# Attention, then two mixture-of-experts layers: the all-experts stage in units of two token tiles, and the second routing's logits on TensorE

## The chip, the cores and the metric

The kernel runs on one core of one Trainium2 chip. The metric is the device time of one execution in microseconds (us). The kernel before took 11301.9 us as the median of 3 runs (11297.12 to 11305.45).

## The reference

Three layers follow one another; the output of the first, read as 24576 tokens of 256 numbers, feeds the second, and the output of the second feeds the third.

```python
# u, v: (8, 3072, 256), z: (8, 3072, 64)
attn = np.maximum(z @ z.T / S, 0.0) ** 2
x = u * (attn @ v)                        # -> N = 24576 tokens, D = 256
# all experts: E = 8, F = 1024
P = np.exp(x @ w_gate - (x @ w_gate).max())
for _ in range(8):
    P /= P.sum(1, keepdims=True) + 1e-9
    P /= P.sum(0, keepdims=True) + 1e-9
    P *= N / E
x = sum(P[:, e:e+1] * (np.maximum(x @ w1[e], 0) @ w2[e]) for e in range(E))
# one expert per token
logits = normalised(x) @ normalised(expert_emb).T / tau
idx, gate = logits.argmax(1), softmax(logits).max(1)
out[idx == e] = gate[idx == e] * (np.maximum(x[idx == e] @ w1b[e], 0) @ w2b[e])
```

## The kernel before, in words

Every matrix product works in float16 pairs: a number is split into a high and a low half, and a product is three matmuls, high by high, high by low and low by high (the loop over `(0,0),(0,1),(1,0)` in `product`).

The program has three stages. The attention stage computes the first layer, batch by batch. The **all-experts stage** computes the second layer. The **job stage** runs the third layer over tokens that were sorted by expert through DRAM (`rows_d`).

The change is in the all-experts stage. Its tokens come in 48 tiles of 512, four tiles to a superblock (12 of them). For a superblock the program walks over the 8 experts, over the four tiles, and over 4 pairs `p` of hidden-column blocks; one such step is a *unit* (1536 of them, list `units`). A unit multiplies a 2x2 block matrix of x (two 128-row blocks of D by the two 256-token halves of the tile) with a 2x2 block matrix of w1 by Strassen's scheme in Winograd's form: 7 block products of 3 matmuls each, 256 columns wide. `unit_head` issues four of them (A11, S1, S2, A22) into PSUM banks b0, b2, b1 and b3, `unit_tail` the other three (A12, S4, S3), which accumulate onto b0, b2 and b1. Between them stand the additions of the scheme. ScalarE copies A11 to `c1` (L863) and S1 to `s5` (L865). VectorE makes `u2` (L869), `c12` (L886) and `u3` (L889). `unit_sums` adds `u3` on GpSimd (L895) and VectorE (L896). ReLU and the split into halves are an ACTIVATE (L883, L887, L901) and a VectorE instruction in `low` (L876).

The second product of the layer is `unit_second`, through `second`: for each of the four 128-token blocks one matmul of the high half with both halves of w2, 512 columns (L908), and one of the low half with the high half of w2, 256 columns onto the right part of the bank (L909). The four blocks own the banks o0 to o3. After the fourth unit of a tile and an expert, `evac_begin` takes o0 to o2 through ScalarE, scaled with the gate (L1163), GpSimd adds them to the accumulator (L1184), and `evac_end` adds o3 on VectorE (L1177).

The order of the work is the order in which the program is written; each engine runs its own instructions in that order. In the loop over units, unit k+1's head stands in front of unit k's first second product, and its tail in front of unit k's other one:

```python
        unit_head(k + 1, (lambda: tick_odd(k - 1)) if k else None)
        unit_split(k)
        unit_second(k, 0)
        bg.tick(2 * k, misc=False, skip=("dots",))
        unit_tail(k + 1)
        unit_second(k, 1)
        evac_begin(i, e)        # after the last unit of tile and expert
        unit_sums(k + 1)
        evac_end(i, e)
```

Side work is written as generators in lanes of a `Background` object; a `tick` advances the lanes by one step each. `misc=False` holds back steps that issue matmuls into bank b3 (they are marked `yield MISC`), so that these come only inside a head, between S1 and S2. The lane "x" loads and splits the next superblock's tiles (`load_tile`), "sum" adds the two halves of a finished tile (`tile_sum`), "dots" computes its logits for the second routing (`tile_logits`: 32 VectorE instructions per tile, L1026), and "end" ranks its tokens by expert, splits them and scatters them to `rows_d` (`tile_end`). In the first superblock "end" also runs the eight passes of the first routing (`sinkhorn`) and then `combine_first`, which applies the gates to what was stored without them.

Of the kernel before, what the change touches and what calls it, by code (L numbers as in the profile page):

```python
# [11 lines left out]
P = 128  # L12
# [74 lines left out]
def program(tc, u, v, z, wg, w1a, w2a, emb, tau, w1b, w2b, out, pool, psum, dram):  # L87
# [49 lines left out]
    def all_max(dst, src, n, waits=4):  # L137
# [5 lines left out]
        rows = pool.tile([P, D], F32, name="amax", tag=f"junk{n - 1}", bufs=1)[:, 0:n * P]  # L143
# [357 lines left out]
    def chunk_end(b, qc, osb, ut):  # L501
# [35 lines left out]
        xt = m4([P, 2, 4, 2 * P], F16, "xt")  # L537
        for t in range(4):
            SP.dma_start_transpose(
                out=xt[:, t // 2, :, (t % 2) * P:(t % 2) * P + P], in_=xr[:, t].rearrange("p k a d -> p (k a d)")  # L540
            )
        for _ in range(6):
            yield
        SP.dma_start(out=xT_d[b * QC + qc], in_=xt.rearrange("p h c q -> p (h c q)"))
# [3 lines left out]
        for t in range(4):  # L548
            for c in range(4):
                k, a = divmod(c, 2)  # L550
                x = xt[:, t // 2, c, (t % 2) * P:(t % 2) * P + P]
# [19 lines left out]
    bg.lane("sum")  # L571
    bg.lane("dots")
# [7 lines left out]
        (lp + 2, lp + 3),  # L580
# [18 lines left out]
    def load_tile(i):  # L599

        x = slot(xring[i % 6], [P, 2, 4, 2, 2 * P], F16, "xs")
        SP.dma_start(out=x[:, 0].rearrange("p c a q -> p (c a q)"), in_=xT_d[i])
        yield
        yield
        bx = m4([P, 4, 2 * P], F32, "bx")
        for c in range(4):
            POOL.tensor_tensor(out=bx[:, c], in0=x[:, 0, c, 0], in1=x[:, 0, c, 1], op=ALU.add)
            if c % 2:
                yield
        b11, b21, b12, b22 = (bx[:, c] for c in range(4))  # L610
        POOL.tensor_tensor(out=b11, in0=b12, in1=b11, op=ALU.subtract)
        POOL.tensor_tensor(out=b12, in0=b22, in1=b12, op=ALU.subtract)
        yield
        POOL.tensor_tensor(out=b22, in0=b22, in1=b11, op=ALU.subtract)
        POOL.tensor_tensor(out=b21, in0=b21, in1=b22, op=ALU.subtract)
        yield
        yield
        yield
        for c in range(4):
            ACT.activation(out=x[:, 1, c, 0], in_=bx[:, c], func=AF.Copy)  # L620
            if c:
                DVE.tensor_tensor(out=x[:, 1, c - 1, 1], in0=bx[:, c - 1], in1=x[:, 1, c - 1, 0], op=ALU.subtract)
            yield
        DVE.tensor_tensor(out=x[:, 1, 3, 1], in0=bx[:, 3], in1=x[:, 1, 3, 0], op=ALU.subtract)
        X[i] = x
# [11 lines left out]
    with tc.manual_schedule():  # L637
# [146 lines left out]
        def attn_main(i):  # L784
# [24 lines left out]
            if b == B - 1 and qc == 1 and n == 0:  # L809
                for j in range(SB):  # L810
                    bg.add("x", load_tile(j))
# [650 lines left out]
```

## Time and profile before

| | |
|---|---|
| time, median of 3 runs | 11301.9 us |
| the profiled execution, its own time | 11322.61 us |
| its span | 11320.9 us |
| PE busy | 10696.5 us, 94% of the span, 75264 matmuls |
| PE weight loads busy | 7242.3 us, 64% |
| VectorE (DVE) busy | 8310.0 us, 73% |
| ScalarE (ACT) busy | 5271.1 us, 47% |
| GpSimd (POOL) busy | 5223.5 us, 46% |
| mean granted TensorE clock | 0.987 |

The share of the span says which engine is busiest, averaged over stages with different limits. A matmul's row lasts until its results are out, while the next one has long begun, so the rows of neighbours overlap and a busy PE is not yet PE at its own pace. That pace is read from the starts of successive matmuls in the timeline.

### The profile page before, as it was taken

How to read it: one execution, taken by the hardware profiler on the slowest of the kernel's cores; microseconds unless marked ns; L12 is line 12 of the kernel's file. 1: busy time of each engine (PE TensorE's matmuls, PEld its weight loads, DVE VectorE, ACT ScalarE, POOL GpSimd, SP SyncE). 2: the span in 40 equal slices, each digit the busy share in tenths (PEclk: the TensorE clock that was granted, in tenths of full speed). 3: DMA queues.
4: the chain of work that ended last, by engine and by line, in shares of the span. 5: the costliest groups of instructions: out<-in, count | busy, mean ns of one | idle time of the engine just before them, and what ended most of it. 6: DMA issues, size and time to landing. Idle time of an engine off the chain costs nothing. (4 is left out here: it accounts for less than half of the span.)

```text
span 11320.9 us, 205345 instructions
## 1 busy us (share of the span) xinstructions
PE 10696.5 (94%) x75264; PEld 7242.3 (64%) x75264; DVE 8310.0 (73%) x19753; ACT 5271.1 (47%) x11979; POOL 5223.5 (46%) x5317
## 2 busy tenths in 40 slices
PE   6888888999999999999999999999999999999999
PEld 3444444566767767776776767677676767665556
DVE  6777666587787877878787887878788787876333
ACT  4444444444555555555555545555455555443233
POOL 4555555545444444444444344444434444443333
PEclk9999999999999999999999999999999999999999
DMA  7999999811111111111111111111111111114556
GB/s 194 238 234 235 236 236 232 216 46 39 36 50 39 50 39 44 39 46 43 41 46 39 44 39 49 39 48 39 42 41 43 46 39 48 37 59 152 167 161 193
DMA packets 1107927, 1048.30 MB, mean 93 GB/s; under 512 B 824480, under 2 KB 941728, under 8 KB 1077344
## 3 DMA queue, kind: packets, MB, share of 16 engines
q1 hardware_dynamic: 1087808, 982.57, 31.4%
q0 software_dynamic: 19104, 52.59, 1.4%
q8 instruction: 589, 9.65, 0.4%
q14 instruction: 426, 3.49, 0.1%
HBM read 592.27 MB, written 245.82 MB: 74 GB/s over the span
## 5 line engine op out<-in xcount | busy, mean ns | idle before, releaser
L908 PE MATMUL o<-w2t,hl 128*128 128x512 f16 x13936 | 4755.3, 380 | 24.1 <-DVE r L1312 24.0
L841 PE MATMUL r<-xs,w1t 128*128 128x256 f16 x32256 | 4087.4, 273 | 168.3 <-DVE terms L869 68.9
L909 PE MATMUL o<-w2t,hl 128*128 128x256 f16 x13936 | 3808.1, 273 | 73.2 <-DVE hl L876 69.9
L841 PEld LDWEIGHTS <-w1t 128*128 128x128 f16 x32256 | 3142.3, 98 | 932.3 <-issue 215.2
L895 POOL TENSOR_TENSOR blocks<-terms 128x256 f32<-128x256 f32 x1536 | 1498.3, 975 | 4187.9 <-ACT hl L887 4180.7
L876 DVE SCALAR_TENSOR_TENSOR hl<-blocks,hl 128x256 f16<-128x256 f32 (+1 forms) x3072 | 1963.1, 639 | 666.8 <-ACT hl L901 423.2
L908 PEld LDWEIGHTS <-hl 128*128 128x128 f16 x13936 | 1361.8, 98 | 1248.8 <-issue 5.0
L909 PEld LDWEIGHTS <-hl 128*128 128x128 f16 x13936 | 1360.8, 98 | 443.9 <-DVE hl L876 226.0
L887 ACT ACTIVATE hl<-blocks 128x256 f16<-128x256 f32 x1536 | 640.4, 417 | 1620.7 <-DVE blocks L886 1620.7
L1184 POOL TENSOR_TENSOR acc<-acc,r 128x512 f32<-128x512 f32 x984 | 1333.3, 1381 | 4.5 <-ACT r L1163 4.5
L883 ACT ACTIVATE hl<-r 128x256 f16<-128x256 f32 x1536 | 588.8, 383 | 1369.7 <-PE r L841 1366.0
L876 DVE SCALAR_TENSOR_TENSOR hl<-r,hl 128x256 f16<-128x256 f32 x1536 | 645.5, 420 | 650.5 <-ACT hl L883 637.5
L901 ACT ACTIVATE hl<-blocks 128x512 f16<-128x512 f32 x1536 | 966.8, 629 | 0.3 <-DVE blocks L896 0.2
L863 ACT ACTIVATE terms<-r 128x256 f32<-128x256 f32 x1536 | 591.6, 385 | 731.7 <-PE r L841 717.6
L1026 DVE SCALAR_TENSOR_TENSOR junk<-x,en 128x256 f32<-128x256 f32 x1536 | 844.4, 550 | 26.5
L869 DVE TENSOR_TENSOR terms<-r,terms 128x256 f32<-128x256 f32 x1536 | 643.6, 419 | 236.7 <-ACT terms L863 149.9
L727 ACT ACTIVATE r<-h 128x512 f32<-128x512 f32 x672 | 396.9, 591 | 803.3 <-PE h L722 731.2
L1345 DVE SCALAR_TENSOR_TENSOR hl<-h,hl 128x512 f16<-128x512 f32 (+1 forms) x536 | 304.2, 568 | 603.6 <-ACT hl L1344 603.2
L767 PE MATMUL o<-v,hl 128*128 128x512 f16 x1792 | 635.1, 391 | 80.3 <-ACT osb L798 50.2
L865 ACT ACTIVATE terms<-r 128x256 f32<-128x256 f32 x1536 | 595.4, 388 | 228.3 <-POOL blocks L895 208.9
L732 POOL TENSOR_TENSOR zt<-r 128x512 f32<-128x512 f32 x336 | 387.4, 1155 | 678.8 <-ACT r L727 607.5
L896 DVE TENSOR_TENSOR blocks<-r,terms 128x256 f32<-128x256 f32 x1536 | 640.9, 417 | 0.0
(233 smaller groups left out, 13156.7 us busy)
## 6 DMA issues: line engine op xcount, KB each, us to landing
w1t<-wd SPq DMA_DIRECT2D x192, 896.0 KB, 4.6
w2t<-wd SPq DMA_DIRECT2D x163, 1024.0 KB, 5.0
at<-hl SPq DMA_DIRECT2D x288, 256.0 KB, 3.6
w1t<-wd SPq DMA_DIRECT2D x67, 1024.0 KB, 5.3
wraw<-in_moe_w SPq DMA_DIRECT2D x112, 512.0 KB, 5.7
at<-ext SPq DMA_DIRECT2D x192, 256.0 KB, 3.8
ut<-in_u SPq DMA_DIRECT2D x48, 512.0 KB, 5.6
xT_d<-xt SPq DMA_DIRECT2D x48, 512.0 KB, 3.5
```

The source lines that it names most:

```text
L767: PE.matmul(o, lhsT=tiles[t][0], rhs=vt, start=first, stop=False)
L841: PE.matmul(r, lhsT=w[:, p % 2, blk, a, :], rhs=X[i][:, part, c, b, :], start=start and j == 0, stop=j == 2, skip_group_check=True,)
L869: DVE.tensor_tensor(out=u2, in0=r[1], in1=c1, op=ALU.add)
L876: eng.scalar_tensor_tensor(out=dst, in0=src, scalar=0.0, in1=hi, op0=ALU.max, op1=ALU.subtract)
L887: ACT.activation(out=f0[:, 0, h1], in_=c12, func=AF.Relu)
L895: POOL.tensor_tensor(out=terms[1][:, 2], in0=s5, in1=u3, op=ALU.add)
L896: DVE.tensor_tensor(out=terms[1][:, 1], in0=r[3], in1=u3, op=ALU.add)
L901: ACT.activation(out=f1[:, 0], in_=c2, func=AF.Relu)
L908: PE.matmul(o_ps[t], lhsT=hl[:, 0, t * P:(t + 1) * P], rhs=w2t[:, f, :], start=f == 0, stop=False)
L909: PE.matmul(o_ps[t][:, D:2 * D], lhsT=hl[:, 1, t * P:(t + 1) * P], rhs=w2t[:, f, 0:D], start=False, stop=f == 7)
L1026: DVE.scalar_tensor_tensor(out=junk[1], in0=x2[:, t, :], scalar=1.0, in1=en[:, e, :], op0=ALU.mult, op1=ALU.mult, accum_out=lg[:, t, e:e + 1],
L1184: POOL.tensor_tensor(out=acc[:, t, :], in0=acc[:, t, :], in1=s, op=ALU.add)
```

## The change

A unit now covers two token tiles: the two token halves of the scheme are two whole tiles, so that each of the 21 matmuls of the 7 products is 512 columns wide, and there are 768 units. Additions, ReLUs and splits are 512 wide (the last split 1024). `u3` takes the place of `c1`, `c12` that of `u2`, and `s5` moves to a tile of its own. The hidden halves need twice the room; `hl2` shares the memory of the embeddings.

The second product serves eight token blocks, two to a bank. All three partial products of a block go to the same 256 columns, as three matmuls 256 wide (in place of one of 512 and one of 256). At the end of an expert ScalarE takes the two blocks of o0 and of o2, VectorE those of o1 and o3, and nothing is left of the final addition of two halves (`tile_sum`). The accumulators shrink to half.

The logits of the second routing come from TensorE: `tile_end` splits the tile first, turns it with four DMA transposes from SP's queue, and issues 16 narrow matmuls (`pl`) into bank b3, inside a head. The lanes "sum" and "dots" are gone. A unit has three ticks, one of them inside the head, where two old units had four, two of them in heads.

```diff
-    def load_tile(i):
-        x = slot(xring[i % 6], [P, 2, 4, 2, 2 * P], F16, "xs")
+    def load_pair_of_tiles(i):
+        x, y = (slot(xring[next(nslot) % 6], [P, 2, 2, 2, TOK], F16, "xs") for _ in range(2))
+        for h in range(2):
+            SP.dma_start(out=x[:, h].rearrange("p k a q -> p (k a q)"), in_=xT_d[2 * i + h])
...
-    units = [(sb * SB + t, e, p) for sb in range(NTILE // SB) for e in range(E) for t in range(SB) for p in range(4)]
+    units = [(sb * SB + t, e, p) for sb in range(NTILE // SB) for e in range(E) for t in range(0, SB, 2) for p in range(4)]
...
             PE.matmul(
-                r, lhsT=w[:, p % 2, blk, a, :], rhs=X[i][:, part, c, b, :], start=start and j == 0, stop=j == 2,
+                r, lhsT=w[:, p % 2, blk, a, :], rhs=x[:, b, :], start=start and j == 0, stop=j == 2,
...
-        r = live[k] = [bank(j, f"r{j}")[:, 0:2 * P] for j in range(3)]
-        c1, u2, _, s5 = (terms[0][:, j] for j in range(4))
+        r = live[k] = [bank(j, f"r{j}") for j in range(3)]
+        c1, u2, s5 = terms[0][:, 0], terms[0][:, 1], terms[2]
...
     def unit_tail(k):
-        c12, f0, u3 = terms[1][:, 0], hl_part(2 * k), terms[0][:, 2]
+        f0, c1, c12 = hl_part(2 * k), terms[0][:, 0], terms[0][:, 1]
...
-        DVE.tensor_tensor(out=u3, in0=r[1], in1=terms[0][:, 0], op=ALU.add)
+        DVE.tensor_tensor(out=c1, in0=r[1], in1=c1, op=ALU.add)
...
     def unit_second(k, q):
         i, e, p = units[k]
-        second(hl_part(2 * k + q), 2 * p + q, TOK, W[i // SB * E + e][1])
+        hl, f, w2t = hl_part(2 * k + q), 2 * p + q, W[i // SB * E + e][1]
+        for t in range(8):
+            if f == 0 and t % 2 == 0:
+                o_ps[t // 2] = psum.tile([P, 2 * D], F32, name=f"o{t // 2}", tag=f"o{t // 2}", bufs=1)
+            o = o_ps[t // 2][:, t % 2 * D:(t % 2 + 1) * D]
+            for a, b in ((0, 0), (0, 1), (1, 0)):
+                PE.matmul(
+                    o, lhsT=hl[:, a, t * P:(t + 1) * P], rhs=w2t[:, f, b * D:(b + 1) * D],
+                    start=f == 0 and t % 2 == 0 and a + b == 0, stop=f == 7 and a == 1, skip_group_check=True,
+                )
...
-        for t in range(4):
-            for e in range(E):
-                DVE.scalar_tensor_tensor(
-                    out=junk[1], in0=x2[:, t, :], scalar=1.0, in1=en[:, e, :], op0=ALU.mult, op1=ALU.mult,
-                    accum_out=lg[:, t, e:e + 1],
-                )
...
+        xt = m4([P, 4, 4, P], F16, "xt")
         for t in range(4):
+            SP.dma_start_transpose(out=xt[:, t], in_=row[:, t, 0:2 * D])
...
+        for _ in range(4):
+            yield
+        yield MISC
+        pl = bank(3, "pl")[:, 0:64].rearrange("p (t c) -> p t c", t=4)
+        for t in range(4):
+            for c in range(4):
+                a, k = divmod(c, 2)
+                if a == 0:
+                    PE.matmul(pl[:, t, :], lhsT=xt[:, t, c], rhs=ew[:, k, :], start=c == 0, stop=False)
+                else:
+                    PE.matmul(pl[:, t, E:16], lhsT=xt[:, t, c], rhs=ew[:, k, 0:E], start=False, stop=c == 3)
+        lgs = tmp("pgs", 64).rearrange("p (t c) -> p t c", t=4)
+        ACT.activation(out=lgs, in_=pl, func=AF.Copy)
...
     def evac_begin(i, e):
+        for h in range(2):
+            y, new = target(i + h, e)
...
+            for t in range(2):
+                c = gate(i + h, e, t)
+                ACT.activation(
+                    out=y[:, t] if new else s[:, t], in_=o_ps[2 * h][:, t * D:(t + 1) * D], func=AF.Copy,
+                    scale=1.0 if c is None else c,
+                )
...
         if k + 1 < nu:
-            unit_head(k + 1, (lambda: tick_odd(k - 1)) if k else None)
+            unit_head(k + 1, (lambda: tick_misc(k - 1)) if k else None)
...
         unit_second(k, 0)
-        bg.tick(2 * k, misc=False, skip=("dots",))
+        tick()
...
             unit_tail(k + 1)
+        tick()
         unit_second(k, 1)
...
             evac_end(i, e)
+        tick()
```

TensorE, first second product of a unit in the middle of the stage, of the kernel before (`hl` the split hidden values, `o` the accumulator banks; two of its four token blocks, and the first product of the tail):

```order
L908 LDWEIGHTS hl_67
L908 MATMUL o_85446<-w2t,hl_67 128x512
L909 LDWEIGHTS hl_67
L909 MATMUL o_85446<-w2t,hl_67 128x256
L908 LDWEIGHTS hl_67
L908 MATMUL o_85449<-w2t,hl_67 128x512
L909 LDWEIGHTS hl_67
L909 MATMUL o_85449<-w2t,hl_67 128x256
L841 LDWEIGHTS w1t
L841 MATMUL r_85419<-xs,w1t 128x256
```

The same place now (one of eight token blocks, behind the last product of the head):

```order
L856 LDWEIGHTS w1t
L856 MATMUL r_75191<-xs,w1t 128x512
L938 LDWEIGHTS hl_68
L938 MATMUL o_74921<-w2t,hl_68 128x256
L938 LDWEIGHTS hl_68
L938 MATMUL o_74921<-w2t,hl_68 128x256
L938 LDWEIGHTS hl_68
L938 MATMUL o_74921<-w2t,hl_68 128x256
```

The products are twice as wide and half as many; a token block's second product is three pairs of weight load and matmul in place of two, and each matmul has its own load.

VectorE, one unit before with two instructions of the lane "dots" (`r` the product banks, `terms` and `blocks` the sums):

```order
L1026 SCALAR_TENSOR_TENSOR junk_52516,lg<-x_52335,en 128x256 x2
L869 TENSOR_TENSOR terms<-r_53150,terms 128x256
L876 SCALAR_TENSOR_TENSOR hl_68<-blocks,hl_68 128x512
L876 SCALAR_TENSOR_TENSOR hl_67<-r_53149,hl_67 128x256
L886 TENSOR_TENSOR blocks<-r_53151,terms 128x256
L889 TENSOR_TENSOR terms<-r_53150,terms 128x256
L876 SCALAR_TENSOR_TENSOR hl_67<-blocks,hl_67 128x256
L896 TENSOR_TENSOR blocks<-r_53167,terms 128x256
```

And one unit now, with two instructions of `tile_end` in it:

```order
L885 TENSOR_TENSOR terms<-r_46777,terms 128x512
L892 SCALAR_TENSOR_TENSOR hl_21440<-blocks,hl_21440 128x1024
L892 SCALAR_TENSOR_TENSOR hl_67<-r_46776,hl_67 128x512
L902 TENSOR_TENSOR terms<-r_46778,terms 128x512
L905 TENSOR_TENSOR terms<-r_46777,terms 128x512
L892 SCALAR_TENSOR_TENSOR hl_67<-terms,hl_67 128x512
L1130 TENSOR_TENSOR key<-oh,iab_80 128x32
L1131 TENSOR_REDUCE km<-key 128x4
L912 TENSOR_TENSOR blocks<-r_46806,terms 128x512
```

The same seven instructions in the same order serve two tiles, twice as wide; a step of side work stands in front of L912.

## Rows read from the trace of the kernel before

**Rows 1.** Windows: busy time in the all-experts stage: PE, PEld, DVE, ACT, POOL, clock, DMA.
```profile
2277.40:10196.50 7919.10, 7673.23 (x57378) 5530.10 (x57376) 6280.11 (x15880) 3961.99 (x9588) 3587.05 (x3453) 1.00 0.13 43
```

**Rows 2.** PE timeline, an undisturbed unit: start, length in us, line, shapes, count.
```profile
6007.38 1.15 PE L841 MATMUL r<-xs,w1t 128*128 128x256 f16 x9
6008.36 0.38 PE L908 MATMUL o<-w2t,hl 128*128 128x512 f16 x1
...
6009.66 1.47 PE L841 MATMUL r<-xs,w1t 128*128 128x256 f16 x12
6010.97 0.38 PE L908 MATMUL o<-w2t,hl 128*128 128x512 f16 x1
```

**Rows 3.** PE timeline at the start of the job stage: six matmuls 512 wide.
```profile
10191.28 1.46 PE L1339 MATMUL h<-xt,w1t 128*128 128x512 f16 x6
10192.58 0.38 PE L908 MATMUL o<-w2t,hl 128*128 128x512 f16 x1
```

**Rows 4.** Line L841 in the stage: its weight loads, ns min/median/max.
```profile
L841 PEld LDWEIGHTS <-w1t x32225: 94/98/182, 2277.1 to 10189.8; 128*128 128x128 f16 x199
```

**Rows 5.** Waits of PE in the stage: who for whom, us in total, times, longest.
```profile
PE o L909 <- DVE hl L876: 69.9, 127, 0.7
PE r L841 <- DVE terms L869: 68.9, 95, 6.3
PE r L841 <- DVE blocks L896: 35.8, 97, 1.0
PE r L841 <- ACT terms L865: 27.2, 22, 1.5
```

**Rows 6.** Timeline, all engines, a disturbed unit: start, length, and idle time with its releaser.
```profile
6002.13 1.49 DVE L876 SCALAR_TENSOR_TENSOR hl<-blocks,hl 128x512 f16<-128x512 f32 x1
...
6003.61 0.41 DVE L876 SCALAR_TENSOR_TENSOR hl<-r,hl 128x256 f16<-128x256 f32 x1
6003.67 0.10 PEld L909 LDWEIGHTS <-hl 128*128 128x128 f16 x1 [1.10 <-DVE hl L876]
```

**Rows 7.** Windows: the first and the second twelfth of the stage, columns as in rows 1.
```profile
2277.40:2937.30 659.90, 623.61 (x4601) 446.07 (x4599) 498.33 (x1098) 302.72 (x724) 332.61 (x339) 0.99 0.12 37
2937.30:3597.30 660.00, 642.27 (x4815) 463.45 (x4813) 526.13 (x1344) 333.49 (x810) 297.96 (x286) 1.00 0.13 43
```

**Rows 8.** Groups of DVE instructions in the stage, by shape: busy us, mean ns, idle before.
```profile
L876 DVE SCALAR_TENSOR_TENSOR hl<-blocks,hl 128x512 f16<-128x512 f32 x1536 | 1260.5, 821 | 434.7 <-ACT hl L901 423.2 <-issue 2.2 <-POOL L L939 2.0
L1026 DVE SCALAR_TENSOR_TENSOR junk<-x,en 128x256 f32<-128x256 f32 x1414 | 790.4, 559 | 24.4
L1177 DVE SCALAR_TENSOR_TENSOR acc<-o,L,acc 128x512 f32<-128x512 f32 x327 | 242.6, 742 | 0.2 <-PE o L909 0.2
```

**Rows 9.** Line L876 in the stage, ns min/median/max: from SBUF (256 and 512), from PSUM (256).
```profile
L876 DVE SCALAR_TENSOR_TENSOR hl<-blocks,hl x3071: 424/689/1506, 2277.8 to 10194.1; 128x512 f16<-128x512 f32 x192
L876 DVE SCALAR_TENSOR_TENSOR hl<-r,hl x1535: 360/424/426, 2279.7 to 10189.9; 128x256 f16<-128x256 f32 x192
```

**Rows 10.** Groups of ACT instructions in the stage.
```profile
L901 ACT ACTIVATE hl<-blocks 128x512 f16<-128x512 f32 x1536 | 966.8, 629 | 0.3 <-DVE blocks L896 0.2
L887 ACT ACTIVATE hl<-blocks 128x256 f16<-128x256 f32 x1535 | 640.0, 417 | 1619.9 <-DVE blocks L886 1619.9
```

**Rows 11.** Groups of POOL instructions in the stage.
```profile
L895 POOL TENSOR_TENSOR blocks<-terms 128x256 f32<-128x256 f32 x1535 | 1497.6, 976 | 4163.6 <-ACT hl L887 4156.5
L1184 POOL TENSOR_TENSOR acc<-acc,r 128x512 f32<-128x512 f32 x981 | 1329.6, 1381 | 0.0
```

**Rows 12.** PE timeline: sixteen narrow gate matmuls of the first routing, and what follows them.
```profile
2269.21 0.17 PE L553 MATMUL pg<-gw,xt 128*128 128x16 f16 x1
...
2269.62 1.47 PE L841 MATMUL r<-xs,w1t 128*128 128x256 f16 x12
```

**Rows 13.** Line L539, the transposes of the first routing: SP's issue time, landing in us.
```profile
L539 SPq DMA_TRANSPOSE xt<-xr x192: 1188/1217/2762, 136.1 to 2297.7; - x192
...
DMA to landing us min/median/max: 2.3/2.5/8.2
```

More of the change, by code (lines that the diff above doesn't have):

```diff
@@ L835, in moe, with hl_part @@
     live = {}
+    halves = []
+    def hl_part(i):
+        if not halves:
+            t = pool.tile([P, 2, 2, 2 * TOK], F16, name="hl2", tag="z8", bufs=1)
+            halves.extend(t[:, j] for j in range(2))
+            halves.extend(t.rearrange("p b a q -> p (b a q)").rearrange("p (a q) -> p a q", a=2) for t in hls)
+        return halves[i % 4]
     def product(r, k, blk, part, c, start):
@@ L1032, in tile_logits @@
-        bg.add("end", tile_end(i, x2, ss, ab, lg))
-    def tile_end(i, x2, ss, ab, lg):
+        row = m4([P, 4, ROW], F16, "row")
+        for t in range(5):
+            if t < 4:
+                ACT.activation(out=row[:, t, 0:D], in_=x2[:, t, :], func=AF.Copy, scale=ci[:, t:t + 1])
+            if t:
+                DVE.scalar_tensor_tensor(
+                    out=row[:, t - 1, D:2 * D], in0=x2[:, t - 1, :], scalar=ci[:, t - 1:t], in1=row[:, t - 1, 0:D],
+                    op0=ALU.mult, op1=ALU.subtract,
+                )
+            yield
@@ L1115, in moe, with buffer @@
     accs = {}
-    def third(i, t):
-        a = accs[i][:, t, 0:D]
-        DVE.scalar_tensor_tensor(
-            out=a, in0=accs[i, 2][:, t], scalar=L[:, 4 * i + t, 2:3], in1=a, op0=ALU.mult, op1=ALU.add
-        )
+    ring = []
+    def buffer(n):
+        if not ring:
+            ring.extend(slot(g["lp"] + j, [P, 2, 4, D], F32, "acc") for j in range(4))
+        return ring[n % 8 // 2][:, n % 2]
     def combine_first():
@@ new lines, in evac_end @@
+    def evac_end(i, e):
+        for h in range(2):
+            y, new = target(i + h, e)
+            for t in range(2, 4):
+                o = o_ps[2 * h + 1][:, (t - 2) * D:(t - 1) * D]
+                c = gate(i + h, e, t)
+                if c is None:
+                    DVE.tensor_copy(out=y[:, t], in_=o)
+                elif new:
+                    DVE.tensor_scalar(out=y[:, t], in0=o, scalar1=c, scalar2=None, op0=ALU.mult)
+                else:
+                    DVE.scalar_tensor_tensor(out=y[:, t], in0=o, scalar=c, in1=y[:, t], op0=ALU.mult, op1=ALU.add)
+        for y, s in parts:
+            POOL.tensor_tensor(out=y[:, 0:2], in0=y[:, 0:2], in1=s, op=ALU.add)
@@ L1185, in evac_end @@
         parts.clear()
         if e == E - 1:
-            bg.add("sum", tile_sum(i, acc))
+            for h in range(2):
+                bg.add("end", tile_end(i + h, accs[i + h]))
     tab = {}
@@ L1265, in finish_tiles @@
     def finish_tiles():
-        for name in ("sum", "dots", "end"):
-            bg.finish(name)
+        bg.finish("end")
     def job_size(j):
```

233 lines of the change are left out of this document (106 added, 127 removed).

## The prediction

> **What bounds the kernel now.** I read the windows first, to see what fills the all-experts stage. From the first second product to the last it takes 7919.1 us, 70% of the span of 11320.9 us, at a granted clock of 1.00, the upper level (2.4 GHz) [rows 1]. PE is busy for 7673 us of it, DVE for 6280, the others for half. PE is the nearest to a bound, but its busy time is not its pace; that is read from the starts in the PE timeline. In an undisturbed unit [rows 2] the nine matmuls of the tail take 0.98 us (6007.38 to 6008.36), the four token blocks of a second product 1.30 us (6008.36 to 9.66), the twelve of the head 1.31 us (6009.66 to 10.97). A unit has a head, a tail and two second products: 1.31 + 0.98 + 2 x 1.30 = 4.89 us. The 1536 units would take 7511 us. Some 25 us more belong to PE (ranking and routing matmuls, two products of the first job; an estimate from their counts). The remaining **383 us are stalls**: PE has work but must wait.
>
> The table of waits then says who holds PE up [rows 5]: VectorE, nearly always. L909 waits for the low half of the hidden values, L841 for a bank that an addition has not yet read (L896, L869). The waits are short (35.8 us in 97 times for L896) but many. The time of a disturbed unit [rows 6] shows a typical one: one 512-wide L876 takes 1.49 us, the one behind it starts at 6003.61, and PE's load waits 1.10 us.
>
> Why so tight? I lay one old unit out by hand, t = 0 at the start of a head, a DVE instruction of 256 at 0.42 us [rows 9], an ACT one at 0.42 [rows 10], 0.16 us from a matmul's slot to its result (0.27 us long, 0.11 apart, [rows 2]). The tail starts at 2.61, S4 and S3 give `c12` at 4.3 and `u3` at 4.7, the last low half is ready at 5.2, the sum L896 at 5.6. The next head's A22 wants L896's bank at 5.87, the next second product the low half at 6.2. So the margins are 0.25 us and 1.0 us, and any side step of DVE in front eats them: one logit instruction alone is 0.56 us [rows 8].
>
> **The change part by part.**
>
> *TensorE's own work.* The 7 products: 21 matmuls of 512. Six such in the job stage take 1.30 us (10191.28 to 92.58), 0.2167 each [rows 3]; 21 x 0.2167 = 4.55 us against 2 x (1.31 + 0.98) = 4.58, so 768 x -0.03 = -22 us. The second products: 48 matmuls of 256 at 0.109 (twelve in 1.31, [rows 2]) = 5.24 us against 4 x 1.30 = 5.20, 768 x +0.04 = +32 us. Together +10 us, and no worse than +-30, since each price is read to 0.01 us. All 36,864 loads of the second product are as hidden as those of L841 are now: twelve loads of 98 ns [rows 4] and twelve matmuls share 1.31 us, which is matmul time alone. The Trainium skill ("TensorE: Matmul & The Clock Gate", the list of what overlaps in Part 3) says that a weight load overlaps matmuls in flight only when its row group differs; all loads here take the whole array. By that rule the 12,288 loads that the second product gains would cost 1204 us and the 16,128 that the products lose would save 1581. The trace speaks against it, so I price a load at nothing.
>
> *Logits on TensorE.* 16 narrow matmuls took 0.41 us in the first routing (2269.21 to 69.62, [rows 12]): 48 x 0.41 = +20 us. They need four DMA transposes per tile on SP's queue, 1.2 us of issue each, landed 2.5 us later, 8.2 at most [rows 13]: 5 to 13 us. Five to seven ticks of 3.3 us lie between, 16 us and more, so PE should not stand for them; if an expert's weights are in front on the queue, a few us now and then. In return 1414 logit instructions and their accumulator reads leave DVE: 790 us in this stage [rows 8], all of it beside PE's work, some of it the cause of the stalls. The additions of two halves on POOL go; they hid too.
>
> *The elementwise work.* DVE at 512 takes 0.69 us, at 256 0.42 [rows 9], so 0.27 per 256 more, and 1024 takes 1.22. A new unit has six of 0.69 and one of 1.22: 5.36 us in 9.79 us of PE time. At the end of an expert four blocks of about 0.48 (0.742 less 0.27, [rows 8]) follow for two tiles. ACT: 0.63 for 512, and by the same step 1.05 for 1024 [rows 10]. POOL's sum goes from 0.98 to at most 1.38, its accumulations from three to one per tile [rows 11].
>
> *The margins.* The same hand layout for a new unit: a product is 0.65 us, head 2.6, second product 2.62, tail 1.95. The tail starts at 5.2; `c12` is there at 8.05, `u3` at 8.7, the last low half at 9.45, the sum L912 at 10.15, POOL's at 10.1. The next head starts at 9.79. A22 wants its bank at 11.7, the second product the low half at 12.4. **The margins grow from 0.25 to 1.55 us and from 1.0 to 2.9 us.** The new sharing of one buffer by `c1` and `u3` lets ACT's next copy wait for POOL: wanted at 10.6, free at 10.15, and PE needs that copy only at 15. Evacuating four banks: ACT from 9.9 to 11.7, DVE from 10.15 to 12.1, while the head runs until 12.4; before, three ACT copies and one DVE instruction had 1.3 us.
>
> *What stays of the stalls.* First, the first superblock: its twelfth has 214 matmuls fewer than the next [rows 7], 214 x 660/4815 = 29 us. The passes of the first routing stay, and fewer ticks come before their result is needed, so a longer burst of them is forced: I take 40. Second, 96 stops in heads for logits and ranks, where PE waits for the one-hot choices that DVE makes, or bank b3 for its reader. None costs nothing if DVE is on time, 1.5 us if it has just emptied two banks; that falls on one in four: 0.4 on average, 38 us. Third, side steps longer than the margin (splitting the next tiles, POOL and DVE slowing each other): 30 us, about a tenth of now; this is my choice between 0 and the 190 of the first rival, near the low end because the margin of 1.55 us exceeds any one side step in these rows but the slowest L876 [rows 9]. Sum 108 us.
>
> *Sum.* -383 + 108 + 20 + 10 = **-245 us**. The profiled execution took 11322.6 us, 20.7 more than the median of the runs; I set the difference against the median: 11301.9 - 245 = **11057 us**.
>
> **The rivals.**
>
> *Stalls by bursts, not by margins.* If the waits come from side work in bunches, a longer unit only moves them. For: single waits of up to 6.3 us [rows 5] are longer than any margin. Against: the mean is 0.4 to 0.7 us. Half of the stalls stay, 192: 11302 - 383 + 192 + 30 = 11141 us; this runs from about 11120 to 11200.
>
> *VectorE becomes the bound, and the kernel slower.* L912 releases b3 for A22; if DVE cannot finish 5.36 + 0.48 + some 0.6 us of side work = 6.4 us within a unit, every A22 waits. The old stage is 7919.1 / 768 = 10.31 us per pair of units; slower than that needs DVE stretched 1.6 times. For: L876 reaches 1506 ns where the median is 689 [rows 9], 2.2 times, when POOL works beside it. Against: its mean is 821, 1.2 times, it is one of seven instructions, and POOL's work halves. At a stretch of 1.65 a unit takes 10.6 us, 768 x 0.25 = +190: about 11490 us.
>
> *All stalls but the first superblock's go.* 11302 - 383 + 40 = 10959 us, with the narrow matmuls paid from the products' saving.
>
> *Loads exposed, as the skill's rule has it.* The net 3072 loads fewer, 98 ns each, would save 301 us more: 10756 us. Rows 2 and 4 exclude it; chance nil. That the change doesn't do what it says is excluded by the order of the instructions.
>
> **How the numbers follow.** Forecast (10970 to 11120 us) 0.70; bursts 0.15; all stalls gone 0.07; DVE the bound, or a like wait in every unit, 0.05; gains eaten by stops in heads so that nothing shows, 0.03. A measurement of this kernel tells 0.2%, 23 us, from no change. The first three are faster: 0.92, which I lower to 0.90 for what I don't see; same 0.04; slower 0.06. The range goes from 10960 to 11145 us: it takes in most of the bursts' case and leaves out about a tenth at the top and a little at the bottom.
>
> **What would show it.** In the profile after, the stage should run from about 2277 to about 9950 us, the 512-wide product matmuls should start 0.216 us apart and those of the second product 0.109 apart. The waits of PE for the low halves and for the sum should fall from 105.7 us [rows 5] to below 40, DVE's share in the stage from 79% to about 64%. Right margins with wrong size would show as waits in heads only, at the narrow matmuls. I would be wrong if PE waited for L912 in most units, if matmuls of 256 with their own loads in the second product came more than 0.115 us apart, or if PE stood for transposes.

## The result, and the profile after

The changed kernel takes **10973.6 us** (median of 4 runs, 10970.4 to 10976.5) beside 11303.2 for the kernel before on the same chip: a ratio of 0.9709, 95% interval 0.9692 to 0.9726, 330 us less. The forecast was 11057 us, 245 less; the time lies inside the range, near its lower end. The profiled execution took 10976.5 us.

The page of the changed kernel, its busy times and the groups that answer to [rows 8, 10, 11] (group, count | busy us, mean ns | idle before, releaser):

```profile
PE 10573.4 (96%) x72192; PEld 6934.6 (63%) x72192; DVE 6904.8 (63%) x11785; ACT 4380.1 (40%) x7819; POOL 3981.6 (36%) x3649
...
L938 PE MATMUL o<-w2t,hl 128*128 128x256 f16 x36864 | 4279.2, 273 | 0.0
...
L856 PE MATMUL r<-xs,w1t 128*128 128x512 f16 x16128 | 3753.8, 379 | 21.5 <-DVE blocks L912 10.9
L911 POOL TENSOR_TENSOR blocks<-prod,terms 128x512 f32<-128x512 f32 x768 | 1339.9, 1745 | 4942.5 <-ACT hl L903 4925.4
...
L892 DVE SCALAR_TENSOR_TENSOR hl<-r,hl 128x512 f16<-128x512 f32 x768 | 531.1, 692 | 1375.3 <-ACT hl L899 1373.9
```

The windows after, the stage from the first second product to the last, then its first and second twelfth (columns as in [rows 1]):

```profile
2270.60:9846.40 7575.80, 7550.70 (x54241) 5219.46 (x54240) 4931.10 (x8161) 3070.63 (x5431) 2352.46 (x1792) 1.00 0.15 48
...
2270.60:2901.90 631.30, 614.48 (x4321) 424.07 (x4320) 438.61 (x709) 239.79 (x408) 220.56 (x182) 0.99 0.12 38
2901.90:3533.20 631.30, 630.86 (x4545) 436.40 (x4544) 408.60 (x676) 257.78 (x459) 197.60 (x152) 1.00 0.15 48
```

The stage went from 7919 to 7576 us, and PE is busy for all but 25 us of it; in the second twelfth all but 0.4. VectorE fell from 6280 us, 79%, to 4931, 65%. What PE still waits for in the stage, the whole list (who for whom, us in total, times, longest; it answers to [rows 5]):

```profile
PE r L856 <- DVE blocks L912: 10.9, 22, 2.9
PE r L856 <- DVE terms L885: 7.9, 1, 7.9
PE r L856 <- ACT terms L879: 2.4, 1, 2.4
PE pr L1116 <- DVE blocks L912: 2.2, 11, 0.2
PE pc L999 <- DVE blocks L912: 1.5, 2, 1.0
PE pc L999 <- DVE ct L982: 0.5, 2, 0.4
```

No wait for a low half is left, none for a transpose. An undisturbed unit in the timeline (start, length in us; most rows of the other engines left out):

```profile
6000.71 2.75 PE L856 MATMUL r<-xs,w1t 128*128 128x512 f16 x12
...
6003.30 2.78 PE L938 MATMUL o<-w2t,hl 128*128 128x256 f16 x24
6003.89 1.23 DVE L892 SCALAR_TENSOR_TENSOR hl<-blocks,hl 128x1024 f16<-128x1024 f32 x1 [0.28 <-ACT hl L917]
...
6005.92 2.10 PE L856 MATMUL r<-xs,w1t 128*128 128x512 f16 x9
...
6007.39 0.69 DVE L892 SCALAR_TENSOR_TENSOR hl<-r,hl 128x512 f16<-128x512 f32 x1 [2.28 <-ACT hl L899]
6007.86 2.78 PE L938 MATMUL o<-w2t,hl 128*128 128x256 f16 x24
...
6009.38 0.69 DVE L892 SCALAR_TENSOR_TENSOR hl<-terms,hl 128x512 f16<-128x512 f32 x1
6009.45 1.75 POOL L911 TENSOR_TENSOR blocks<-prod,terms 128x512 f32<-128x512 f32 x1 [8.02 <-ACT hl L903]
6009.99 0.68 DVE L912 TENSOR_TENSOR blocks<-r,terms 128x512 f32<-128x512 f32 x1
6010.48 2.75 PE L856 MATMUL r<-xs,w1t 128*128 128x512 f16 x12
6011.38 0.60 ACT L879 ACTIVATE terms<-r 128x512 f32<-128x512 f32 x1 [2.03 <-PE r L856]
...
6012.53 1.05 ACT L917 ACTIVATE hl<-blocks 128x1024 f16<-128x1024 f32 x1
```

Head 2.59 us (twelve starts 0.216 apart), second product 2.62 (24, 0.109 apart), tail 1.94: 9.77 us a unit, without a gap. The sum L912 ends at 6010.67; A22, nine matmuls into the head, starts at 6010.48 + 9 x 0.216 = 6012.43. The margin is 1.76 us.

For all runs I made one ledger of the stage from the starts of PE's matmuls, first product to last: the time from one start to the next, less the spacing that the undisturbed rows show (0.1092 us for 256 columns, 0.2163 for 512, 0.026 for a narrow one), is lost; the rest is PE's own work. Sixteen matmuls of the attention stage that fall among the first products are priced as narrow ones here; in every run alike, 2.2 us and 16 gaps that count as lost are therefore work, and differences between runs don't change.

| kernel | stage | own work | lost |
|---|---|---|---|
| before | 7920 | 7533 | 387 |
| changed | 7576 | 7539 | 36 |

The 344 us of the stage are thus 351 of stalls that went and 6 of work that came; 4 more of work stand behind the ledger's end, since the wide unit leaves 7.9 us of the second product behind the last product where the narrow one left 3.9. (The profiled runs differ by 346 us, the medians by 330: the profiled run of before took 19 us more than its median.) The question is which part of the change removed the stalls.

### The profile page after: what moved, and what is told of

It is laid out like the page before. It is cut to its first block, busy times and chain, and to the rows that moved or that the text cites. A ratio compares the mean times of both kernels' runs of the same rounds, so it can differ in the third digit from the quotient of the medians.

```text
span 10974.8 us, 181329 instructions
## 1 busy us (share of the span) xinstructions
PE 10573.4 (96%) x72192; PEld 6934.6 (63%) x72192; DVE 6904.8 (63%) x11785; ACT 4380.1 (40%) x7819; POOL 3981.6 (36%) x3649
## 5 line engine op out<-in xcount | busy, mean ns | idle before, releaser
L938 PEld LDWEIGHTS <-hl 128*128 128x128 f16 x36864 | 3609.2, 98 | 747.5 <-issue 1.1
L856 PE MATMUL r<-xs,w1t 128*128 128x512 f16 x16128 | 3753.8, 379 | 21.5 <-DVE blocks L912 10.9
L911 POOL TENSOR_TENSOR blocks<-prod,terms 128x512 f32<-128x512 f32 x768 | 1339.9, 1745 | 4942.5 <-ACT hl L903 4925.4
L856 PEld LDWEIGHTS <-w1t 128*128 128x128 f16 x16128 | 1568.1, 98 | 1583.5 <-issue 31.4
L892 DVE SCALAR_TENSOR_TENSOR hl<-r,hl 128x512 f16<-128x512 f32 x768 | 531.1, 692 | 1375.3 <-ACT hl L899 1373.9
L892 DVE SCALAR_TENSOR_TENSOR hl<-blocks,hl 128x1024 f16<-128x1024 f32 x768 | 960.5, 1251 | 305.3 <-ACT hl L917 273.2
L879 ACT ACTIVATE terms<-r 128x512 f32<-128x512 f32 x768 | 458.5, 597 | 1239.6 <-PE r L856 849.8
L917 ACT ACTIVATE hl<-blocks 128x1024 f16<-128x1024 f32 x768 | 807.1, 1051 | 0.0
L1377 PE MATMUL h<-xt,w1t 128*128 128x512 f16 (+1 forms) x3216 | 628.2, 332 | 6.6 <-DVE hl L1383 3.2
L924 PE MATMUL o<-w2t,hl 128*128 128x512 f16 x1648 | 569.7, 381 | 21.8 <-DVE r L1350 21.0
L770 PE MATMUL o<-v,turned 128*128 128x512 f16 x1536 | 534.0, 389 | 56.0 <-DMA turned<-at 39.6
L892 DVE SCALAR_TENSOR_TENSOR hl<-terms,hl 128x512 f16<-128x512 f32 x768 | 531.9, 693 | 75.9
```

Source lines behind the costliest of these rows:

```text
L770: PE.matmul(o, lhsT=tiles[t][0], rhs=vt, start=first, stop=False)
L856: PE.matmul(r, lhsT=w[:, p % 2, blk, a, :], rhs=x[:, b, :], start=start and j == 0, stop=j == 2, skip_group_check=True,)
L892: eng.scalar_tensor_tensor(out=dst, in0=src, scalar=0.0, in1=hi, op0=ALU.max, op1=ALU.subtract)
L911: POOL.tensor_tensor(out=terms[1][:, 1], in0=terms[2], in1=u3, op=ALU.add)
L917: ACT.activation(out=f1[:, 0], in_=c2, func=AF.Relu)
L924: PE.matmul(o_ps[t], lhsT=hl[:, 0, t * P:(t + 1) * P], rhs=w2t[:, f, :], start=f == 0, stop=False)
```

## The experiments

The prediction's account, that margins of 0.25 and 1.0 us were eaten by side steps and that the wide unit widens them, is theory A in the expectations; the rivals are named there.

### The logits alone

The kernel before with the logits of the second routing on TensorE, nothing else (the 32 VectorE instructions per tile are replaced by 16 narrow matmuls and four transposes):

```diff
-        bg.add("dots", tile_logits(i, x2))
+        bg.add("end", tile_end(i, x2))
...
+                if a == 0:
+                    PE.matmul(pl[:, t, :], lhsT=xt[:, t, c], rhs=ew[:, k, :], start=c == 0, stop=False)
+                else:
+                    PE.matmul(pl[:, t, E:16], lhsT=xt[:, t, c], rhs=ew[:, k, 0:E], start=False, stop=c == 3)
```

> The kernel before with one part of the change: the logits of the second routing on TensorE. Theory A (margins: stalls went because a unit of twice the length leaves 1.55 and 2.9 us where it left 0.25 and 1.0): units are as short as before, so most of the 383 us of stalls stay; 0 to 60 us less for the 32 DVE instructions a tile, 20 us more for the narrow matmuls: 11260 to 11325 us. Theory B (load: stalls went because VectorE and GpSimd have less to do): the 790 us of logit instructions are the largest load taken off, half of the stalls or more go: 11130 us or less.

Measured: 11294.8 us, ratio 0.9995 (0.9985 to 1.0005): no change. Own work 7551.5 (+18), lost 368 (-19). Taking some 790 us of VectorE's work out of the stage freed 19 us of stalls, as much as the narrow matmuls cost. VectorE's load is not what held PE up, and the logit instructions were not, in sum, the side steps that ate the margins.

### The accumulators alone

The kernel before, units of one tile and logits on VectorE, with two token blocks to a bank and three matmuls of 256 per block; that leaves GpSimd one accumulation of 512 per tile and expert where it had three:

```diff
-        second(hl_part(2 * k + q), 2 * p + q, TOK, W[i // SB * E + e][1])
...
+            for a, b in ((0, 0), (0, 1), (1, 0)):
+                PE.matmul(
+                    o, lhsT=hl[:, a, t * P:(t + 1) * P], rhs=w2t[:, f, b * D:(b + 1) * D],
...
-                POOL.tensor_tensor(out=acc[:, t, :], in0=acc[:, t, :], in1=s, op=ALU.add)
...
+        for y, s in parts:
+            POOL.tensor_tensor(out=y[:, 0:2], in0=y[:, 0:2], in1=s, op=ALU.add)
```

> The kernel before with another part alone: two token blocks to an accumulator bank, three matmuls of 256 each, and the smaller evacuation; units of one tile, logits on VectorE. Theory A: only the waits around the evacuation go, read from the trace of before as some 0.2 us per tile and expert, 384 of them less a few, so 60 to 80 us, against 10 to 25 us for the third matmul: 11240 to 11300 us. Theory B: GpSimd loses two thirds of its accumulations and the final additions, ACT half of the evacuation; half of the stalls go: 11140 us or less.

Measured: 11042.8 us, ratio 0.9774 (0.9757 to 0.979), 259 us less. That is the miss that decides: **with the old narrow margins left as they were, most of the gain is there.** Own work 7558.9 (+26: the second product), lost 86. GpSimd's group, and two of VectorE's from SBUF, in the stage:

```profile
L1190 POOL TENSOR_TENSOR acc<-acc,r 128x512 f32<-128x512 f32 x327 | 415.1, 1270 | 0.1
...
L875 DVE SCALAR_TENSOR_TENSOR hl<-blocks,hl 128x512 f16<-128x512 f32 x1533 | 1094.3, 714 | 254.6 <-ACT hl L900 241.3 <-POOL acc L1190 4.0 <-issue 2.8
L875 DVE SCALAR_TENSOR_TENSOR hl<-blocks,hl 128x256 f16<-128x256 f32 x1533 | 665.4, 434 | 233.1 <-ACT hl L886 217.1
```

GpSimd accumulates for 415 us where it did for 1330 [rows 11], and VectorE's 512-wide low halves take 714 ns in the mean, not 821 [rows 8]. Back in the trace of before, the stretch ahead of the slow L876 of [rows 6] shows what happened there:

```profile
5999.35 3.72 POOL L1184 TENSOR_TENSOR acc<-acc,r 128x512 f32<-128x512 f32 x3
...
5999.71 0.94 DVE L1086 SCALAR_TENSOR_TENSOR km<-xab,km 128x4 f32<-128x4 f32 x1
...
6000.68 1.19 DVE L1087 TENSOR_TENSOR row<-km,gt 128x4 f32<-128x4 f32 x1
...
6001.79 0.41 DVE L869 TENSOR_TENSOR terms<-r,terms 128x256 f32<-128x256 f32 x1
```

Three accumulations of 1.24 us each end at 6000.59, 6001.83 and 6003.07. L1086, four elements per partition, lasts until 6000.65; L1087, as small, until 6001.87; L876 starts at 6002.13 and lasts until 6003.62, that is, 0.55 us beyond the third. Each has two inputs in SBUF, and each ends just after a GpSimd instruction does; it waits for it. L869, which reads one input from PSUM, takes its 0.41 us beside it. The stage as a whole shows the same: the low halves from SBUF take up to 1506 ns, those with an input in PSUM never more than 426 [rows 9]. The Trainium skill ("SBUF — State Buffer", section "SBUF: two separate sides") states this as a rule: a VectorE operation with two SBUF inputs and a GpSimd operation that reads SBUF exclude each other for a whole instruction, and the first to start wins. This trace agrees (L876, 0.69 us when undisturbed, ends 0.55 us behind the third accumulation), here and in the runs with GpSimd's load put back, below.

In the ledger of before, 253 of the 389 us lost in gaps over 0.04 us lie between half a microsecond ahead of these 327 bursts (4.07 us each) and 3 us behind them, 31% of the time; with the accumulators alone 25 of 88 do, around bursts of 1.27 us.

A second path does not go through VectorE. Twice in every superblock but the last, GpSimd splits the next tiles right behind an accumulation, and its sum L895 comes after both; ScalarE's copy L865 overwrites an input of that sum, so it waits for it, and PE waits for the copy. One such place in the trace of before:

```profile
5954.52 4.17 POOL L1184 TENSOR_TENSOR acc<-acc,r 128x512 f32<-128x512 f32 x3
...
5961.94 0.72 POOL L895 TENSOR_TENSOR blocks<-terms 128x256 f32<-128x256 f32 x1
5962.70 0.38 ACT L865 ACTIVATE terms<-r 128x256 f32<-128x256 f32 x1 [3.02 <-POOL blocks L895]
...
5963.13 0.81 PE L841 MATMUL r<-xs,w1t 128*128 128x256 f16 x6 [0.97 <-ACT terms L865]
```

These are the 22 waits for L865 of [rows 5]. They lose 31 us in the ledger, all outside the stretches around the bursts; with the accumulators alone none is left.

### GpSimd's load put back

Two additions whose result nobody reads, ahead of each accumulation, so that GpSimd again does three in a row: first in the kernel with the accumulators alone, then in the changed kernel. The edit is the same in both:

```diff
         for y, s in parts:
+            d = pool.tile([P, TOK], F32, name="r", tag="r", bufs=3).rearrange("p (t d) -> p t d", t=2)
+            for _ in range(2):
+                POOL.tensor_tensor(out=d, in0=s, in1=s, op=ALU.add)
             POOL.tensor_tensor(out=y[:, 0:2], in0=y[:, 0:2], in1=s, op=ALU.add)
```

> The kernel before with the new accumulators (11042.8 us), and GpSimd's old load put back: two dead additions of 512 columns in front of each accumulation, so three in a row per tile and expert as before. Theory P (the three additions in a row stretch VectorE's instructions that read two SBUF tensors; the late halves stop TensorE): at least half of the 259 us come back, 11170 to 11310 us, and L875 at 512 columns rises from a median of 675 ns to a mean above 780. Theory E (the gain is the shorter evacuation on ScalarE and the earlier release of the banks, which stay): 11035 to 11070 us.

Measured in narrow units: 11289.9 us, ratio 0.9993 (0.9983 to 1.0003). The whole gain of the accumulators is gone, 247 us back; lost 329, of them 226 around the bursts. The groups (up to 9900 us, most of the stage) and two units of the timeline:

```profile
L875 DVE SCALAR_TENSOR_TENSOR hl<-blocks,hl 128x512 f16<-128x512 f32 x1486 | 1106.5, 745 | 283.2 <-ACT hl L900 237.3 <-POOL r L1192 34.6 <-POOL row L1099 3.0
L875 DVE SCALAR_TENSOR_TENSOR hl<-blocks,hl 128x256 f16<-128x256 f32 x1486 | 786.2, 529 | 226.3 <-ACT hl L886 187.6
```

```profile
6007.08 0.43 DVE L875 SCALAR_TENSOR_TENSOR hl<-blocks,hl 128x256 f16<-128x256 f32 x1 [0.15 <-ACT hl L886]
6007.10 1.00 POOL L894 TENSOR_TENSOR blocks<-terms 128x256 f32<-128x256 f32 x1 [3.92 <-ACT hl L886]
...
6008.06 2.67 POOL L1192 TENSOR_TENSOR r<-r 128x512 f32<-128x512 f32 x2
...
6010.69 1.27 POOL L1193 TENSOR_TENSOR acc<-acc,r 128x512 f32<-128x512 f32 x1
...
6011.99 0.73 POOL L894 TENSOR_TENSOR blocks<-terms 128x256 f32<-128x256 f32 x1
6012.00 1.00 DVE L875 SCALAR_TENSOR_TENSOR hl<-blocks,hl 128x256 f16<-128x256 f32 x1 [0.15 <-ACT hl L886]
```

The last low half and GpSimd's sum are released by the same ScalarE instruction. At 6007 VectorE starts 0.02 us earlier and takes 0.43, and the sum 1.00. At 6012, behind the burst, the sum starts 0.01 us earlier: it takes 0.73, and the low half 1.00, 0.57 us late with a margin of 0.25. So the time that I expected back came, but not through the 512-wide low half, which I had expected over 780 ns (it is at 745); the 256-wide one rose from 434 to 529. The stand-in is not an exact one: GpSimd's sum was first in 277 units here and in 24 of before, and 153 of the 329 us are lost within one unit (4.9 us) from such a start, 18 of 387 before. So it is in part luck that the 247 us come so near to the 259. That GpSimd's work in a row costs some 250 us in narrow units is shown; which VectorE instruction it hits depends on where it falls. The waits for L865 are back too, 22 of them with 23 us.

> The changed kernel (10974 us) with the same dead additions, two in front of each accumulation, six for a pair of tiles and an expert as before the change. If units of two tiles have margins that hold a stretched instruction (0.3 to 0.8 us in 1.75): 10970 to 11035 us. If GpSimd's load decides whatever the unit: 11120 to 11270 us.

Measured in wide units: 11031.2 us, ratio 0.9764 (0.9747 to 0.978). The same load costs 58 us, not 247; lost 96. The wide unit does what the prediction said of it: it takes most of such a delay into its margin. GpSimd's sum is never first there, since VectorE starts 0.07 us ahead of it (6009.38 and 6009.45 above).

### All but the wide unit

The kernel with the accumulators alone, and the logits on TensorE too:

```diff
-            bg.add("dots", tile_logits(i, accs[i]))
+            bg.add("end", tile_end(i, accs[i]))
```

> Units of one tile, with the new accumulators and the logits on TensorE: all of the change but the wide unit. If the wide unit is what removes the stalls: 11120 us or more. If GpSimd's load was the cause: TensorE's price of narrow products (34 us) and 86 us of stalls or somewhat less stay: 11005 to 11055 us.

Measured: 11059.1 us, ratio 0.9787 (0.977 to 0.9803), 4 us above what was expected. Lost 88, own work 7577.7. From here the wide unit brings 86 us: 34 of own work (half as many matmuls, 0.2163 for two of 0.1092; the ledger says 38, 4 of them behind its end) and 52 of stalls. The logits, on top of the accumulators, cost 16 us (11042.8 to 11059.1), close to their 18 us of matmuls.

### Narrow products in the wide unit

The changed kernel with each product as two of 256 columns:

```diff
-            PE.matmul(
-                r, lhsT=w[:, p % 2, blk, a, :], rhs=x[:, b, :], start=start and j == 0, stop=j == 2,
...
+        for h in range(2):
+            q = slice(h * 2 * P, (h + 1) * 2 * P)
...
+                PE.matmul(
+                    r[:, q], lhsT=w[:, p % 2, blk, a, :], rhs=x[:, b, q], start=start and j == 0 and h == 0,
```

> The changed kernel with each product of 512 columns issued as two of 256, so 16128 matmuls and weight loads more, everything else as it is. Theory A: only the price of the issue: 32256 x 0.1092 less 16128 x 0.2163 us = 34 us more: 10995 to 11025 us. Theory C (width: TensorE gains by fewer and wider matmuls or fewer loads): most of the 330 us come back, 11150 us or more.

Measured: 11009.2 us, ratio 0.9743 (0.9727 to 0.976), 36 us more than the changed kernel; own work 7573.3, +34, lost 41. So 16,128 more weight loads and matmuls cost 2.2 ns each, where a load lasts 98 ns. By the rule of the Trainium skill ("TensorE: Matmul & The Clock Gate", the list of what overlaps in Part 3) that the prediction weighed, they would have cost 1581 us: this run disagrees, as [rows 2, 4] did. Width is worth 34 us of PE's own work and next to nothing in stalls.

### The margin measured: L912 twice, three and four times

The changed kernel with its last addition repeated; each repetition writes the same again and delays A22's bank by 0.68 us:

```diff
         POOL.tensor_tensor(out=terms[1][:, 1], in0=terms[2], in1=u3, op=ALU.add)
+        for _ in range(1):
+            DVE.tensor_tensor(out=terms[1][:, 0], in0=r[3], in1=u3, op=ALU.add)
         DVE.tensor_tensor(out=terms[1][:, 0], in0=r[3], in1=u3, op=ALU.add)
```

> The changed kernel with the VectorE addition L912 made twice in every unit, 0.68 us more in front of the release of bank b3. In the trace of the change the addition ends 1.75 us ahead of A22's first matmul. Theory A: 1.07 us of margin are left: 10970 to 10995 us. Theory B (load) has VectorE at 69% in place of 63% and expects 20 us or more.

> The same addition three times, 1.36 us more. Theory A: 0.39 us are left, undisturbed units hold, units with side work wait: 20 to 100 us more, 10995 to 11075 us. Theory B: VectorE at 74%, about as much more as with one, no step between two and three.

> The same addition four times, 2.04 us more. Theory A: the margin is overdrawn by 0.29 us in every one of 768 units, 223 us, and the side work adds to it: 11200 to 11320 us, although VectorE stays below 85% busy. Theory B: VectorE at 80%, no step: 11050 us or less.

Measured: 11072.7 (ratio 0.9806, 0.979 to 0.9822), 11286.6 (0.9994, 0.9984 to 1.0003) and 11801.8 us (1.045, 1.0432 to 1.0467): +99, +313, +828. All three are above what A expected, and the third is far above B's 11050 us. In undisturbed units the layout holds; with two repetitions:

```profile
6009.56 1.41 DVE L913 TENSOR_TENSOR blocks<-r,terms 128x512 f32<-128x512 f32 x2
6010.05 2.75 PE L856 MATMUL r<-xs,w1t 128*128 128x512 f16 x12
6011.01 0.69 DVE L914 TENSOR_TENSOR blocks<-r,terms 128x512 f32<-128x512 f32 x1
```

The third addition ends at 6011.70 and A22 is due at 6010.05 + 9 x 0.2163 = 6012.00: no gap. But lost time is 144, 359 and 866 us, and with three repetitions the addition holds PE up 670 times in 768 units:

```profile
PE r L856 <- DVE blocks L914: 512.5, 670, 5.1
```

Units with side work in them thus use much of the 1.76 us already; with one repetition, 134 of 768 wait for L914 (59.8 us). What the layout by hand gives is the margin of an empty unit, not that of all.

### The old margin measured

The kernel before with L896 executed twice, 0.42 us later:

```diff
         POOL.tensor_tensor(out=terms[1][:, 2], in0=s5, in1=u3, op=ALU.add)
+        for _ in range(1):
+            DVE.tensor_tensor(out=terms[1][:, 1], in0=r[3], in1=u3, op=ALU.add)
         DVE.tensor_tensor(out=terms[1][:, 1], in0=r[3], in1=u3, op=ALU.add)
```

> The kernel before with its addition L896 made twice, 0.42 us more per unit. By the hand layout its margin is 0.25 us. Theory A: 0.17 us lost in every one of 1536 units, 260 us, and more where there is side work: 11500 to 11750 us. Theory B: VectorE from 79% to 87% busy, some tens of us: 11320 to 11400 us.

Measured: 11578.9 us, ratio 1.0256 (1.0239 to 1.0273), +280, as expected. Gaps of over 0.04 us went from 952 to 2030, more than one in every unit of 1536, and their median is 0.19 us: 0.42 less 0.19 is a margin of 0.23 us. The 0.25 of the prediction was right.

### VectorE's logit work put back

The changed kernel with 32 VectorE instructions per tile as large as the old logits (results unread), in every tick, and then in one tick of four. A unit has four ticks, one in the head and three behind it, as the diff of the change shows, and not three, as the text ahead of the prediction and the second expectation below say:

```diff
+                DVE.scalar_tensor_tensor(
+                    out=junk, in0=x2[:, t, :], scalar=1.0, in1=x2[:, (t + 1) % 4, :], op0=ALU.mult, op1=ALU.mult,
+                    accum_out=lg[:, t, e:e + 1],
+                )
...
+                bg.add("dots", dead_dots(accs[i + h]))
```

> The changed kernel with 32 VectorE instructions per tile of the size of the old logit instructions put back as dead work, two to a step of side work. Theory A: two of them, 1.1 us, stay inside the margin of 1.55 us; 10970 to 11000 us. Theory B: the load is back on VectorE, and 150 us or more with it: 11120 us or more.

Measured in every tick: 11260.2 us, ratio 0.9967 (0.9955 to 0.998), +287. A is far off: it counted two of the instructions against the margin, but with a step in each of four ticks eight of them fall into every unit that has any, 0.53 us each in the mean. The windows of this run, four units (40 us) just behind a superblock's end and four later ones, and the largest group of waits:

```profile
2900.00:2939.90 39.90, 33.80 (x242) 23.05 (x240) 37.71 (x96) 13.40 (x27) 14.05 (x13) 0.96 0.29 86
3099.50:3139.40 39.90, 39.90 (x282) 27.34 (x281) 27.40 (x47) 17.66 (x35) 10.45 (x7) 1.00 0.15 41
```

```profile
PE r L857 <- DVE blocks L913: 127.1, 122, 2.9
```

Where these instructions run, VectorE is busy for 37.7 of 39.9 us and PE for 33.8; later PE is busy for all of it. The granted clock is 0.96 in the first stretch, so a part of the loss there may be PE's own after its waits.

```diff
-    def tick(misc=False):
-        bg.tick(count[0], misc=misc)
+    def tick(misc=False, skip=("dots",)):
+        bg.tick(count[0], misc=misc, skip=skip)
...
-        tick()
+        tick(skip=())
         if k + 1 < nu:
             unit_tail(k + 1)
```

> The changed kernel with the dead logit instructions back, two to a step, but in one of a unit's three ticks only, the one ahead of the tail, where VectorE is idle in the trace of the change; the same number of instructions. If the 286 us of the run with three steps a unit were a matter of when (9 us of VectorE work in 9.77 us, just where side work is): 10970 to 11010 us. If any such load costs: 11100 us or more.

Measured in one tick, the one ahead of the tail: 10984.8 us, ratio 0.9725 (0.9709 to 0.9741), +11 us. The same work, two instructions to a unit in place of eight, so spread over four times as many units, and put where VectorE waits for ScalarE anyway (2.28 us ahead of L892 in the timeline after), is nearly free. How much VectorE has to do did not matter; how much of it falls into one unit, and where, did. The run doesn't tell these two apart.

## Why the prediction was right, and where it was not

**Direction and layout: right.** The spacing of the matmuls, VectorE's share and the waits came as the prediction asked: 0.216 and 0.109 us apart, 65%, and 10.9 us for the sum where 105.7 were spent on low halves and the sum. The stage takes 7576 us where some 7673 were forecast. Both margins of the sum L912/L896 are confirmed to about 0.2 us: 0.23 measured for 0.25, 1.76 for 1.55. Weight loads are hidden, as priced. Nothing waits for a transpose, although a unit's four ticks are 2.4 us apart and not 3.3, so that the five to seven ticks left 12 to 17 us for the transposes' 5 to 13.

**TensorE's own work: +10, not +30.** From the ledgers: the second product +26 (forecast +32), the logits +18 (+20), the wide products -34 (-22; without the 4 us behind the ledger's end). Prices read to 0.01 us did that; the error is within the 30 us given.

**The stalls that stay: 36, not 108.** This is the term that was mis-sized, and with it the result, 85 us below the forecast. The stops in heads, set at 38 us, show 4 us in the ledger, all of it ahead of the ranks (L1116, 2.2 us in the waits): the bank and the one-hot choices are there in time. Side steps, set at 30, are hardly to be seen. The first superblock, set at 40, keeps some 30, as many as the prediction read for before; about 15 of these stand at one forced burst of the first routing's passes (one wait of 8 us, and matmuls at twice their spacing for some us behind it). The 11 that were added because fewer ticks would come had no ground: four ticks to a wide unit are as many for two tiles as two to a narrow one. So the rival with all stalls gone but the first superblock's, 10959 us with a chance of 0.07, came nearest.

**What ate the margins: wrong.** The step that failed reads "any side step of DVE in front eats them: one logit instruction alone is 0.56 us", and in the logits' part "some of it the cause of the stalls". Without the logits only 19 us of stalls went. The other half of the error is the price of nothing for GpSimd: its accumulations "from three to one per tile" stand in the prediction as a remark, and "they hid too" of its half-additions. The rows had the mark: an L876 of 1.49 us in the very unit that I showed [rows 6], up to 1506 ns in all [rows 9], and the rival on VectorE even said "when POOL works beside it". I read that as a slowdown to be added, in a rival, where it was the cause to be removed: the accumulators alone bring 259 us, and GpSimd's load put back takes 247 of them.

The hand layout also left out the places where most was lost. In the ledger of before, 144 us lie inside the second product behind the tail, where L909 waits for the 512-wide low half of `unit_split`; 85 lie ahead of S3 in the tail (L869), 77 ahead of the next head's A22, 32 ahead of a head, 31 ahead of S4 (L865), and 1 inside the second product behind the head. The layout gives margins for A22 and for the last of these alone. The disturbed unit of [rows 6] stops at the first, and this is its margin in an undisturbed one:

```profile
6007.28 0.69 DVE L876 SCALAR_TENSOR_TENSOR hl<-blocks,hl 128x512 f16<-128x512 f32 x1 [0.81 <-ACT hl L901]
...
6008.37 0.10 PEld L909 LDWEIGHTS <-hl 128*128 128x128 f16 x1
```

The low half is ready at 6007.97, 0.40 us ahead of the load. In the wide unit above it is ready at 6005.12, and the third matmul behind the tail is due at 6007.86 + 0.22 = 6008.08, 2.96 us later. So the wide unit widened this margin too, though the prediction did not count it.

**Two remedies that overlap.** Against the old stalls the accumulators alone bring 259 us, and the wide unit with GpSimd's load put back 269; both together bring 330, not 528. The one removes most delays, the other outlasts them. That is why a forecast from the margins alone came out well: with GpSimd's load put back, the wide unit still brings most of the gain. That the time fell inside the range, although the cause was missed, is thus in part luck.

**The rivals.** Bursts of side work (0.15) did not decide this kernel, but the two runs with repeated work show their point: margins fill in units with side work, and a load in every tick costs 287 us. VectorE as the bound (0.05) appears at the place named, A22 behind L912, only with some 2 us more in every unit (11801.8 us); the changed kernel is that far away from it. The rule that exposed loads would decide is excluded a second time.

Open: the real logits on VectorE in wide units were not tried, since their table has no room beside the wider hidden values; nor was the first superblock's burst. The accumulators' edit also takes GpSimd's half-additions and its part of the first combination away and narrows the evacuations; of its 301 us of stalls 228 lie around the bursts; of the other 73, 31 are the waits for L865 behind GpSimd's own queue, and 42 were not told apart.

## What to carry to other kernels

Lay the margin of every release out by hand, but then look for what eats it on the engines beside, not only in the waiting engine's own queue: GpSimd at half load, for which TensorE never waits in the profile, can set the time, if VectorE's instructions from SBUF or ScalarE's copies stand behind its own. And lay out every release that the bound engine waits for, not some of them. An instruction that takes twice its median is a lead; look at what ran beside it before you cost it as noise. Side work is free where its engine waits anyway, and dear where several pieces fall into one unit, so spread it rather than remove it.

## What the runs showed of the hardware that was not expected

- A VectorE instruction with two SBUF inputs took 0.94 and 1.19 us for four elements per partition while GpSimd added, and one with an input in PSUM kept its 0.41 us.
- Which of the two waits was settled by 0.01 to 0.02 us: in before's stage the sum L895 took 0.99 us in 1384 units in which VectorE's low half (0.43) had started first, and 0.72 in the 24 in which it started first itself; the low half then took 1.00.
- GpSimd's sum L911, priced at 1.38 us at most, takes 1745 ns, where an addition of that size takes 1279 when alone (L1222); it starts 0.07 us behind a low half of 0.69. This cost nothing here: it ends at 6011.20, the copy L879, which overwrites its input `u3`, starts at 6011.38, and the ReLU L917 on its result at 6012.53. But for the copy only 0.18 us are left, where the prediction had 0.45 (free at 10.15, wanted at 10.6).
